# Linear attention and 16 routed experts on one core: fewer steps in a routing group, counts in bf16, and a new order of the first stage

## The chip, the cores and the metric

The program runs on one core of one Trainium2 chip. The metric is the device time of one execution in microseconds (us), the median of three runs. TensorE (PE), VectorE (DVE), ScalarE (ACT) and GpSimd (POOL) each work through a queue of their own in program order; SyncE (SP) issues most of the transfers, POOL those that scatter rows by an index.

## The reference, cut to what matters

```python
kv = einsum('bhsd,bhse->bhde', k, v)            # 8 batches, 8 heads, 576 rows, 64 wide
out = einsum('bhsd,bhde->bhse', q, kv)
x = out / sqrt(mean(out * out, -1) + 1e-6) * g_norm   # -> 4608 tokens of 512
g_idx, g_w = argmax and its softmax weight of x @ w_group        # 4 groups
e_idx, e_w = the same of x @ w_expert[g_idx]                     # 4 experts in each
y = g_w * e_w * (relu(x @ w1[g_idx, e_idx]) @ w2[g_idx, e_idx])  # 512 -> 1024 -> 512
```

Everything is float32. Each token goes to one of 16 experts.

## The kernel before, in words

**First stage: attention and routing.** The 4608 tokens are 36 tiles of 128. For each of the 8 batches SP loads k, v and q (8 x 3 MB and small tails, L516 and L528), PE forms kv, and for each tile it forms the tile's output and router logits in one product (L598). ACT copies the output into a ring of 20 tiles (`xo`, L603), copies the logits (L541) and squares the output (L619); DVE sums the squares (L626). Tiles are routed in eight groups (`GS`): DVE and ACT compute 1/rms (L719 to L741), the logits (L751, L756), their maxima and one-hot marks (L762 to L793), the exponentials and the token's weight (L841 to L905). PE sums the one-hot marks into running ranks (`rk`, L802 to L808, with the count so far, `carry`, of float32), DVE turns ranks into row numbers (`keys`, L834), and POOL scatters each tile's rows (544 floats a token, 4 x 136) into a table in memory, `xs`, sorted by expert (L267; a put in what follows). Ahead of most puts POOL writes the token's number into the tile's columns `TOK` and up (L913); groups 3, 4 and 7 do this in one copy a group (L924).

**The early region.** After group 1 the fullest expert is picked. When groups 0 to 4 (24 tiles) have been put, SP reads 256 of this expert's rows back (L292), and while groups 5 to 7 are still routed, PE computes the expert for these 256 tokens (first layer L363, second layer L1258 in nine passes). Its weights come in four loads of 1 MB (L223); the first needs only the pick.

**The order of the first stage** is found by a planner in the kernel itself: each piece of work is a step with an engine, a cost, a rank and the steps that it needs; the planner plays the steps through with its own costs and latencies (`SAME`, `OTHER`), and where several steps of an engine could start, the lowest rank (`RANK`, `ROUTE`, `FOLD`, `LOADS`, ...) goes first. What comes out is the order of each engine's queue. In the planner a put takes 1.28, has its rows in memory 0.1 + 1.0 later, and a step on POOL may follow 1.2 after that. A tile's place in the ring may be written again when the put of the tile 20 before it has landed.

**Between the stages** the rest of the first expert's tokens (region 0, 128 rows) and the preparation of region 1 are written out by hand (from L1462): the read of region 0's rows (`read(0)`, L292 again), the read of region 1's (`read(1)`, L289, which needs the widths of `region_columns`, L1372), the splitting of float32 weights into a high and a low part (ACT L246, DVE L250), the last piece of the early region's second layer (`head_layer2`), region 0's first layer (from `xT`, `xTl`), the row limits (`row_bounds`, `bad`, `ridx`) and masks (`quarter_masks`).

**Second stage.** Regions 1 to 15, one expert each, in three products a tile of weights (L374, L375, L379). The tiles `xh`, `xl`, `hh`, `hl` that PE reads are laid from column 16 x `FIRST_X[r]` or 16 x `FIRST_H[r]` on. At the end the results are scattered into the output, and a loop for overflowing rows is passed by.

## Time and profile before

| | us |
|---|---|
| median of three runs (lowest, highest) | 530.22 (529.77, 530.44) |
| the profiled execution's own time | 530.08 |
| its span, first to last instruction | 528.4 |
| PE busy in the span | 514.4 (97%) |
| DVE, ACT, POOL busy | 398.8, 277.8, 258.3 |

The profiled execution lies 0.14 us under the median, and 1.7 us of its time lie outside the span. PE's busy time includes warming products without use (L447) in the first stage, so that its share does not say what bounds that stage.

### The profile page before, as it was taken

What the parts mean: (1) busy time and instruction counts of PE and PEld (TensorE: products, weight loads), DVE (VectorE), ACT (ScalarE), POOL (GpSimd) and SP (SyncE); (2) the same over time, 40 slices, a digit from 0 to 9 for tenths busy, and PEclk for the clock granted to TensorE, in tenths of its full rate; (3) what the DMA queues carried; (4) which work ended last, traced back from release to release, by engine and by line L of the source; (5) the groups of instructions that cost most, each with busy time, mean ns of one, the idle gap of its engine ahead of it and who ended that gap; (6) DMA issues with size and microseconds to landing.
All of it is one profiled execution on the core that took longest, in us unless ns stands there. A gap on an engine that the chain in (4) does not pass through costs nothing. (4 is left out here: it accounts for less than half of the span.)

```text
span 528.4 us, 12161 instructions
## 1 busy us (share of the span) xinstructions
PE 514.4 (97%) x4262; PEld 497.7 (94%) x4262; DVE 398.8 (75%) x852; ACT 277.8 (53%) x499; POOL 258.3 (49%) x356
## 2 busy tenths in 40 slices
PE   6899999999999999999999999999999999999995
PEld 3899998788899999999999999999999999999995
DVE  4259998978967887887877777877878777878760
ACT  0378888634653544455454454545554646556551
POOL 7002865461021745647584646455564738365271
PEclk9899999999999999999999999999999999999998
DMA  8999998946998374636856555565748384854010
GB/s 319 422 422 418 419 423 325 354 182 208 300 360 320 106 289 125 250 118 174 297 219 198 219 197 222 199 253 158 269 148 306 107 329 124 316 209 182 15 40 36
DMA packets 44026, 126.50 MB, mean 239 GB/s; under 512 B 6992, under 2 KB 26390, under 8 KB 32925
## 3 DMA queue, kind: packets, MB, share of 16 engines
q1 hardware_dynamic: 36029, 105.71, 54.5%
q0 software_dynamic: 7760, 19.48, 10.0%
q8 instruction: 62, 1.02, 0.8%
q14 instruction: 31, 0.25, 0.2%
q10 hardware_dynamic: 144, 0.04, 0.1%
HBM read 105.73 MB, written 20.51 MB: 239 GB/s over the span
## 5 line engine op out<-in xcount | busy, mean ns | idle before, releaser
L1438 POOL DMA_INDIRECT out_dram<-z,idx x140 | 164.3, 1173 | 155.4 <-DVE idx L1416 117.0
L375 PE MATMUL ps<-xl,whi 128*128 128x300 f32 (+12 forms) x480 | 141.5, 295 | 0.0
L374 PE MATMUL ps<-xh,whi 128*128 128x300 f32 (+12 forms) x480 | 141.3, 294 | 0.0
L379 PE MATMUL ps<-xh,wlo 128*128 128x300 f32 (+12 forms) x480 | 141.3, 294 | 0.0
L375 PE MATMUL psy<-hl,w2h 128*128 128x300 f32 (+11 forms) x448 | 133.0, 297 | 0.0
L374 PE MATMUL psy<-hh,w2h 128*128 128x300 f32 (+11 forms) x448 | 132.9, 297 | 0.0
L379 PE MATMUL psy<-hh,w2l 128*128 128x300 f32 (+11 forms) x448 | 132.6, 296 | 0.0
L250 DVE TENSOR_TENSOR wlo<-wr,whi 128x1024 fp32r<-128x1024 f32 x64 | 97.2, 1522 | 22.2 <-ACT whi L246 22.1
L379 PEld LDWEIGHTS ps<-xh,wlo 128*128 128x128 f32 x480 | 90.3, 188 | 0.0
L375 PEld LDWEIGHTS ps<-xl,whi 128*128 128x128 f32 x480 | 90.3, 188 | 0.0
L374 PEld LDWEIGHTS ps<-xh,whi 128*128 128x128 f32 x480 | 90.3, 188 | 0.0
L324 ACT ACTIVATE hh<-ps 128x328 fp32r<-128x328 f32 (+11 forms) x120 | 50.4, 420 | 74.5 <-PE ps L379 73.7
L352 DVE TENSOR_TENSOR w2l<-wr,w2h 128x1024 fp32r<-128x1024 f32 x60 | 73.4, 1224 | 18.9 <-ACT w2h L348 18.1
L379 PEld LDWEIGHTS psy<-hh,w2l 128*128 128x128 f32 x448 | 84.3, 188 | 0.0
L375 PEld LDWEIGHTS psy<-hl,w2h 128*128 128x128 f32 x448 | 84.2, 188 | 0.0
L374 PEld LDWEIGHTS psy<-hh,w2h 128*128 128x128 f32 x448 | 84.2, 188 | 0.0
L348 ACT CAST w2h<-wr 128x1024 fp32r<-128x1024 f32 x60 | 62.5, 1042 | 38.7 <-PE psy L375 35.3
L325 DVE SCALAR_TENSOR_TENSOR hl<-ps,hh 128x328 fp32r<-128x328 f32 (+11 forms) x120 | 55.6, 463 | 23.3 <-ACT hh L324 23.2
L1430 ACT ACTIVATE xh<-xt,rw 128x328 fp32r<-128x328 f32 (+11 forms) x60 | 32.6, 544 | 68.6 <-DVE xt L311 68.6
L246 ACT CAST whi<-wr 128x1024 fp32r<-128x1024 f32 x64 | 66.3, 1037 | 1.3 <-DMA wr<-in_w_dram 1.3
L267 POOL DMA_INDIRECT xs<-xo,keys x36 | 35.7, 991 | 31.4 <-DVE pt L751 10.3
L321 POOL TENSOR_TENSOR xq<-xq 128x1280 f32<-128x1280 f32 (+3 forms) x14 | 33.9, 2419 | 18.1 <-DMA xq<-xs 17.9
(302 smaller groups left out, 671.9 us busy)
## 6 DMA issues: line engine op xcount, KB each, us to landing
wr<-in_w_dram SPq DMA_DIRECT2D x64, 1024.0 KB
m_q<-in_qm_dram SPq DMA_DIRECT2D x8, 1024.0 KB
m_k<-in_k_dram SPq DMA_DIRECT2D x7, 1024.0 KB
m_v<-in_v_dram SPq DMA_DIRECT2D x7, 1024.0 KB
xq<-xs SPq DMA_DIRECT2D x20, 153.0 KB
out_dram<-z,idx POOLq DMA_INDIRECT x140
xq<-xs SPq DMA_DIRECT2D x16, 136.0 KB
xq<-xs SPq DMA_DIRECT2D x12, 119.0 KB
```

What stands on the lines that cost most here:

```text
L246: nc.scalar.copy(out=hi, in_=w)
L250: eng.tensor_tensor(out=lo, in0=w, in1=hi.bitcast(F32), op=ALU.subtract)
L267: sc = nc.gpsimd.indirect_dma_start(out=xs, out_offset=bass.IndirectOffsetOnAxis(ap=keys[:, c:c + 1], axis=0), in_=x.rearrange("p i f -> p ...
L321: eng.tensor_tensor(out=part(x, n), in0=part(x, n), in1=factors(x, n), op=ALU.mult)
L324: nc.scalar.activation(out=hh, in_=ps, func=AF.Relu)
L325: nc.vector.scalar_tensor_tensor(out=hl, in0=ps, scalar=0.0, in1=hh.bitcast(F32), op0=ALU.max, op1=ALU.subtract)
L348: nc.scalar.copy(out=piece(hi, hf, i2), in_=halfpiece(wt[hf][0], i2))
L352: nc.vector.tensor_tensor(out=piece(lo, hf, i2), in0=halfpiece(wt[hf][0], i2), in1=piece(hi, hf, i2).bitcast(F32), op=ALU.subtract)
L374: nc.tensor.matmul(ps, lhsT=stat_h(c), rhs=mov_h(c), start=(c == 0), stop=False)
L375: nc.tensor.matmul(ps, lhsT=stat_h(c), rhs=mov_l(c), start=False, stop=False)
L379: nc.tensor.matmul(ps, lhsT=stat_l(d), rhs=mov_h(d), start=False, stop=(d == n - 1))
L1438: sc = nc.gpsimd.indirect_dma_start(out=out4, out_offset=bass.IndirectOffsetOnAxis(ap=idx[:, g:g + 1], axis=0), in_=z[:, g, :], in_offset= ...
```

## The change

A routing group loses the step `m` (ACT takes the mean and the 1e-6 into the logarithm), the step that adds 1e-9 to `se` (now part of the two steps behind it) and `carry`. The counts so far are kept as bf16 counts a partition (`counted`), summed by one reduction a group, and PE adds them with two bf16 products in place of the float32 one. POOL writes the token numbers of every group in one copy, which needs only that the ring's places are free. The groups are 5 and 3 tiles where they were 4 and 4 (groups 3 and 4). The 256 early rows are read in two transfers, and the first of the expert's weights is loaded behind them. The ranks are new. Between the stages `region_columns` moves into the first stage, `row_bounds` and the masks move behind region 0's products, `head_layer2` gets the bank of `ps_e`, and one weight split goes ahead of `xTl`. `FIRST_X` and `FIRST_H` change in four places, and one constant of 512 bytes a partition is gone, so that the tiles behind it lie elsewhere.

```diff
-FIRST_X = [0, 0, 0, 0, 2, 2, 2, 0, 0, 0, 2, 2, 0, 1, 1, 0]
-FIRST_H = [0, 0, 0, 0, 0, 0, 0, 2, 2, 2, 1, 1, 1, 1, 1, 0]
-
-
-GS = [6, 5, 5, 4, 4, 5, 4, 3]
+FIRST_X = [0, 0, 0, 0, 2, 2, 2, 0, 0, 0, 2, 1, 0, 1, 1, 0]
+FIRST_H = [0, 0, 0, 0, 0, 1, 1, 2, 2, 1, 1, 1, 1, 1, 1, 0]
+
+
+EARLYIDS = -30.0
+
+
+GS = [6, 5, 5, 5, 3, 5, 4, 3]
...
-RANK = {'hl': 25.95, 'wh': 39.35, 'wd': 636.8, 'ek': -2962.18, 'o': 5229.48, 'ok': 34.12, 'sq': 7956.27, 'red': 2.73, 'w': -2197.5, 'wl': 2652.43, 'wl2': -2193.01, 'xt': -587.87, 'xs': 18.38, 'l1': 10123.65, 'hs': -14.64, 'l2': 58.33, 'lk': 9.34}
...
+ROUTE = [0.98, 5.63, -0.45, 4.95, 44.06, 5.6, -21.59, -24.17]
+FOLD = [327.49, -98.1, -44.42, 3.17, 1.83, -24.19, -89.66, -194.68]
...
-    ones_f = cp.tile([1, P], F32, name="ones_f")
+    g2 = cp.tile([P, 1], F32, name="g4")
+    tiny = cp.tile([P, 1], F32, name="tiny")
+    base_b = cp.tile([P, NE], BF16, name="base_b")
...
+    def read_tokens(x, row, nb, eng, head=False, j=0):
+        d = eng.dma_start(x.rearrange("p j i f -> p (j i f)"), xs[bass.ds(row, P * nb), :][j * P:(j + 1) * P])
...
+    ps_e = both.enter_context(tc.tile_pool(name="ps_e", bufs=1, space=bass.MemoryType.PSUM))
...
-                nc.vector.tensor_scalar(out=tl([H], "m"), in0=mss[g][:, 0:nt, :].rearrange("p t h -> p (t h)"),
-                                        scalar1=1.0 / D, scalar2=1e-6, op0=ALU.mult, op1=ALU.add)
-            s = do("D", nt * H, [done["red", c] for c in cols] + [get("end", g - 2)], f)
-
-            def f():
-                nc.scalar.activation(out=tl([H], "lnm"), in_=v["m"], func=AF.Ln)
-            s = do("A", nt * H, [s], f, us=0.25)
+                v["ms"] = mss[g][:, 0:nt, :].rearrange("p t h -> p (t h)")
+                nc.scalar.activation(out=tl([H], "lnm"), in_=v["ms"], func=AF.Ln, scale=1.0 / D, bias=tiny[:, 0:1])
+            s = do("A", nt * H, [done["red", c] for c in cols] + [get("end", g - 2)], f, us=0.25)
...
+                v["seen"] = counted[g % 2]
+                nc.vector.tensor_tensor(out=v["seen"][:, 1:1 + nt, :], in0=v["oh3"],
                                         in1=sign.unsqueeze(1).to_broadcast([P, nt, NE]), op=ALU.mult)
-                v["ohs3"] = v["ohs"].rearrange("p (t e) -> p t e", e=NE)
-            s1 = do("D", nt * 16, [s1, done["constants"]], f)
+            s1 = do("D", nt * 16, [s1, done["constants"], get("rk", g - 2), get("seen", g - 2)], f)
...
                 rk = v["rk"] = ps_r.tile([P, 512], F32, name="rk", tag="psr")
-                nc.tensor.matmul(rk[:, 0:nb_], lhsT=ones_f, rhs=st["carry"].unsqueeze(1).to_broadcast([1, nt + 1, NE]),
-                                 start=True, stop=False)
-                for t in range(nt):
-                    nc.tensor.matmul(rk[:, (t + 1) * NE:nb_], lhsT=ones_b,
-                                     rhs=v["ohs3"][:, t, :].unsqueeze(1).to_broadcast([P, nt - t, NE]), start=False,
-                                     stop=False)
-                nc.tensor.matmul(rk[:, 0:nt * NE], lhsT=upper_b, rhs=v["ohs"], start=False, stop=True)
+                for t in range(-1, nt + 1):
+                    x = base_b if t < 0 else v["seen"][:, t, :]
+                    m = nt + 1 - max(t, 0)
+                    nc.tensor.matmul(rk[:, max(t, 0) * NE:nb_], lhsT=ones_b,
+                                     rhs=x.unsqueeze(1).to_broadcast([P, m, NE]), start=(t < 0), stop=False)
+                nc.tensor.matmul(rk[:, 0:nt * NE], lhsT=upper_b, rhs=v["seen"][:, 1:1 + nt, :].rearrange("p t e -> p (t e)"),
+                                 start=False, stop=True)
                 v["tot"] = rk[:, nt * NE:nb_]
-            rk = do("PE", 0, [s1, done["carry", g - 1], get("kr", g - 1), get("tot", g - 1)], f, us=0.1 + 0.065 * nt)
-
+            rk = done["rk", g] = do("PE", 0, [s1, get("seen", g - 1), get("kr", g - 1), get("tot", g - 1)], f,
+                                    us=0.12 + 0.055 * nt)
+
+            if not last:
+                def f():
+                    with nc.allow_low_precision(reason="a partition's tokens number at most 36"):
+                        nc.vector.tensor_reduce(out=counted[(g + 1) % 2][:, 0, :],
+                                                in_=v["seen"][:, 0:nt + 1, :].rearrange("p t e -> p e t"), op=ALU.add,
+                                                axis=AX.X)
+                done["seen", g] = do("D", nb_, [s1, get("rk", g - 1)], f)
 
             def f():
                 nc.vector.tensor_tensor(out=tl([NE], "kr"), in0=v["rk"][:, 0:nt * NE], in1=v["ohb"], op=ALU.mult)
-            kr = done["kr", g] = do("D", nt * 16, [rk], f)
+            kr = cnt = done["kr", g] = do("D", nt * 16, [rk], f)
...
-                    carry = sm.tile([1, NE], F32, name="carry", bufs=2)
-                    nc.vector.tensor_copy(out=carry, in_=v["tot"][0:1, :])
-                    st["carry"] = carry
-                cnt = done["carry", g] = do("D", NE, [rk], f)
...
-                    nc.vector.tensor_scalar(out=v["se"], in0=v["se"], scalar1=1e-9, scalar2=None, op0=ALU.add)
...
+            eng, e = (nc.vector, "D")
+
+            def f():
+                nc.vector.tensor_reduce(out=tl([5], "se"), in_=v["ex"], op=ALU.add, axis=AX.X)
+                v["se5"] = v["se"].rearrange("p (t s) -> p t s", s=5)
+            w = do("D", nt * 20, [w], f)
+
+            def f():
+                nc.vector.scalar_tensor_tensor(out=tl([1, 4], "s4"), in0=v["se5"][:, :, 1:5], scalar=1e-9,
+                                               in1=v["oh5"][:, :, 0, :], op0=ALU.add, op1=ALU.mult)
+            w = do("D", nt * 4, [w], f)
+
+            def f():
+                nc.vector.tensor_reduce(out=tl([1], "s1_"), in_=v["s4"], op=ALU.add, axis=AX.X)
+            w = do("D", nt * 4, [w], f)
+
+            def f():
+                nc.vector.scalar_tensor_tensor(out=tl([1], "cw"), in0=v["se5"][:, :, 0], scalar=1e-9, in1=v["s1_"],
+                                               op0=ALU.add, op1=ALU.mult)
+            w = do("D", nt, [w], f)
...
-            def put(c):
-                nc.gpsimd.tensor_copy(out=xot[c][:, :, TOK:REC].bitcast(I32),
-                                      in_=tok4[:, c, :].unsqueeze(2).to_broadcast([P, 4, REC - TOK]))
-                put_rows(c, xot[c])
-
-            us = 1.58
-            put_all = last or g in (EARLY - 1, EARLY)
-            if put_all:
-                def f():
-                    for lo, hi in [(0, min(nt, XO - r0)), (min(nt, XO - r0), nt)]:
-                        if hi > lo:
-                            at = (r0 + lo) % XO
-                            nc.gpsimd.tensor_copy(
-                                out=ring[:, at:at + hi - lo, :, TOK:REC].bitcast(I32),
-                                in_=tok4[:, c0 + lo:c0 + hi, :].unsqueeze(3).to_broadcast([P, hi - lo, 4, REC - TOK]))
-                ids = do("G", nt * 60, [done["ok", c] for c in cols], f)
-                us, put = 1.28, lambda c: put_rows(c, xot[c])
+            def f():
+                for lo, hi in [(0, min(nt, XO - r0)), (min(nt, XO - r0), nt)]:
+                    if hi > lo:
+                        at = (r0 + lo) % XO
+                        nc.gpsimd.tensor_copy(
+                            out=ring[:, at:at + hi - lo, :, TOK:REC].bitcast(I32),
+                            in_=tok4[:, c0 + lo:c0 + hi, :].unsqueeze(3).to_broadcast([P, hi - lo, 4, REC - TOK]))
+            ids = step("G", cost("G", nt * 60), cols[0] + EARLYIDS, [get("in", c - XO) for c in cols], f)
 
             for c in cols:
-                prev = do("G", 0, [w, ids if put_all else None, ks, done["sq", c], prev], lambda c=c: put(c), us=us)
+                prev = do("G", 0, [w, ids, ks, done["sq", c], prev], lambda c=c: put_rows(c, xot[c]), us=1.28)
...
+            x = do("D", 32, [x], f, us=0.2)
+            done["srow"] = do("D", 32, [x], region_columns, us=1.0)
             return cnt
 
         def early_region(do, rows):
             xq0 = ap_.tile([P, HEAD // P, 4, REC], F32, name="xq0", bufs=1)
 
-            def f():
-                read_tokens(xq0, first_row(star_row), HEAD // P, nc.sync, head=True)
             s = do("W", 0, rows + [done["star_row"]], lambda: None, us=1.0)
-            s = do("S", 0, [s], f, us=2.8)
+            st["read"] = []
+            for j in range(HEAD // P):
+                def f(j=j):
+                    if j == 0:
+                        st["row"] = first_row(star_row)
+                    read_tokens(xq0[:, j:j + 1], st["row"], HEAD // P, nc.sync, head=True, j=j)
+                s = do("S", 0, [s], f, us=1.41)
+                st["read"].append(s)
...
-                               ([] if i == 0 else [wt[-1], st["read"]]) + [done["star_idx"]], f,
+                               ([] if i == 0 else [wt[-1]]) + [st["read"][-1], done["star_idx"]], f,
...
-                s = step("D", 0.62, r0 + RANK["xt"] + 0.1 * j, [st["read"]], f, take=1 if j == 0 else 0)
+                s = step("D", 0.62, r0 + RANK["xt"] + 0.1 * j, [st["read"][j]], f, take=1 if j == 0 else 0)
...
-            for n, (j, hf, x) in enumerate([(j, 0, x) for x in (0, 2, 1) for j in range(2)] + [(0, 1, x) for x in (0, 2, 1)]):
+            for n, (j, hf, x) in enumerate([(0, 0, 0), (1, 0, 0), (0, 0, 2), (1, 0, 2), (0, 1, 0), (0, 1, 2), (0, 0, 1), (1, 0, 1), (0, 1, 1)]):
...
-                carry = sm.tile([1, NE], F32, name="carry", bufs=2)
-                nc.vector.tensor_copy(out=carry, in_=ekey[0:1, :])
-                st["carry"] = carry
-            done["carry", -1] = done["constants"] = step("D", 0.1, 3, [s], f)
+                for i in range(2):
+                    counted.append(sm.tile([P, GMAX + 1, NE], BF16, name=f"counted{i}"))
+                nc.vector.memset(counted[0][:, 0, :], 0.0)
+                nc.vector.tensor_scalar(out=counted[0][0:1, 0, :], in0=odd[0:1, :], scalar1=-1.0, scalar2=None,
+                                        op0=ALU.mult)
+                nc.vector.tensor_scalar(out=base_b, in0=middle, scalar1=1.0 / P, scalar2=None, op0=ALU.mult)
+            done["seen", -1] = done["constants"] = step("D", 0.3, 3, [s], f)
...
+        psy = [ps_q.tile([P, 512], F32, name=f"psy{d}") for d in range(3)]
+        psy.append(ps_e.tile([P, 512], F32, name="psy3", tag="pse"))
-        region_columns()
...
+        ids0 = mp.tile([P, 1], F32, name="ids0", bufs=1)
+        nc.vector.tensor_copy(out=ids0, in_=xqs[0][:, 0, TOK:TOK + 1])
+        o = psy[3][:, 0:DM // 2]
...
-            split_low(w1r[1], q, nc.vector)
-        row_bounds()
...
+        split_low(w1r[1], 0, nc.vector)
...
+        split_low(w1r[1], 1, nc.vector)
...
-        for _ in quarter_masks():
-            pass
...
+        row_bounds()
+        bad = [mp.tile([P, 3], F32, name=f"bad{i}", bufs=1) for i in range(2)]
...
+        for _ in quarter_masks():
+            pass
```

## Rows read from the trace of the kernel before

**Rows 1.** The profile's page, its second part, DMA busy tenths in 40 slices of 13.2 us.

```profile
DMA  8999998946998374636856555565748384854010
```

**Rows 2.** Windows: start:end, length, then busy us of PE, PEld, DVE, ACT, POOL, PEclk, DMA share, GB/s.

```profile
93.00:103.00 10.00, 9.63 (x60) 6.93 (x55) 9.86 (x46) 6.53 (x17) 4.09 (x7) 1.00 0.97 354
...
140.26:522.56 382.30, 382.30 (x2858) 381.31 (x2856) 292.40 (x464) 192.72 (x297) 200.10 (x156) 1.00 0.57 202
```

**Rows 3.** DMA queues from 3 to 91 us: packets, MB, share.

```profile
q1 hardware_dynamic: 6998, 29.20, 80.9%
q0 software_dynamic: 1920, 6.69, 18.7%
```

**Rows 4.** DMA queue of the puts, from 50 us to 62.79 and to 77.77.

```profile
q0 software_dynamic: 362, 1.28, 24.6%
...
q0 software_dynamic: 1014, 3.56, 31.4%
```

**Rows 5.** Timeline of SP's issues: start us, us, line, transfer.

```profile
58.11 0.35 SPq L223 DMA_DIRECT2D wr<-in_w_dram  x1
...
91.64 0.40 SPq L292 DMA_DIRECT2D xq<-xs  x1
...
118.10 0.34 SPq L292 DMA_DIRECT2D xq<-xs  x1
...
121.87 3.90 SPq L289 DMA_DIRECT2D xq<-xs  x8
```

**Rows 6.** Timeline of POOL: start us, us, line, operation, idle before.

```profile
50.54 1.18 POOL L267 DMA_INDIRECT xs<-xo,keys  x1 [7.66 <-DVE ex L766]
...
77.77 0.97 POOL L267 DMA_INDIRECT xs<-xo,keys  x1 [1.68 <-issue]
...
86.70 0.97 POOL L267 DMA_INDIRECT xs<-xo,keys  x1 [0.30 <-ACT xr L541]
...
99.05 0.22 POOL L913 COPY xo<-tok 128x16 int32<-128x16 int32 x1
...
114.80 0.98 POOL L267 DMA_INDIRECT xs<-xo,keys  x1 [0.30 <-issue]
```

**Rows 7.** Timeline of PE in the early region.

```profile
98.37 5.34 PE L363 MATMUL l<-xx,wr 128*128 128x256 f32 x24
...
103.65 0.44 PE L802 MATMUL rk<-carry,ones_f 1*128 1x80 f32 x2
```

**Rows 8.** Timeline of DVE in the last groups' routing.

```profile
100.72 0.17 DVE L719 TENSOR_SCALAR m<-ms 128x24 f32<-128x24 f32 x1
...
104.51 0.15 DVE L821 COPY carry<-rk 1x16 f32<-1x16 f32 x1
...
104.79 0.21 DVE L834 TENSOR_REDUCE keys<-kr 128x4 int32<-128x64 f32 x1
...
108.53 0.17 DVE L852 TENSOR_SCALAR se<-se 128x15 f32<-128x15 f32 x1
```

**Rows 9.** Timeline of DVE and PE between the stages.

```profile
121.03 0.69 DVE L302 TENSOR_TENSOR xn<-xq 128x512 f32<-128x512 f32 x1 [0.32 <-DMA xq<-xs]
...
123.36 0.39 PE L374 MATMUL ps<-whi,hhi 128*128 128x256 f32 x1 [0.46 <-ACT xx L1276]
...
126.76 0.39 PE L374 MATMUL ps<-lc,lb 128*128 128x512 f32 x1
...
130.81 1.76 DVE L321 TENSOR_TENSOR xq<-xq 128x1536 f32<-128x1536 f32 x1 [0.24 <-DMA wr<-in_w_dram]
...
134.27 0.39 PE L379 MATMUL ps<-whi,la 128*128 128x256 f32 x1 [1.19 <-DVE la L1533]
```

**Rows 10.** Timeline of PE, first products of two regions 300 wide.

```profile
256.18 0.30 PE L374 MATMUL ps<-xh,whi 128*128 128x300 f32 x1
...
269.30 0.30 PE L374 MATMUL psy<-hh,w2h 128*128 128x300 f32 x1
...
282.73 0.30 PE L374 MATMUL ps<-xh,whi 128*128 128x300 f32 x1
```

112 lines of the change are left out of this document (30 added, 82 removed).

## The prediction, made before the changed kernel was run

> **What bounds the kernel now.** I read the page first, then windows by stage, the transfers, and last the timelines around the seam between the stages. [rows 1] show the transfer engines full until about 80 us and then falling. In [rows 2] the second stage, from 140.26 to 522.56 us, has PE busy 382.30 of 382.30 us: no wait is left in it, and the time behind it (528.4 less 522.56, 5.8 us) is the last scatter, which the change doesn't touch. So a gain must bring region 1's first product forward from 140.26, or make the products themselves quicker.
>
> Two chains meet ahead of region 0's first layer, at 126.76 [rows 9].
>
> The first is PE's own: the early region starts at 98.37 [rows 7], 6.7 us after its rows are read at 91.64 [rows 5], and PE has little idle time from there on. The read waits for 24 puts. From 3 to 91 us the queues moved 29.20 MB of loads and 6.69 MB of puts [rows 3], 35.9 MB in 88 us, 0.41 MB/us: they are full, and the last bytes to arrive are those of the puts. One of the 29 MB is the expert's first weight half, issued at 58.11, ahead of the last q [rows 5].
>
> The second is that of the last put: issued at 114.80 [rows 6], followed by the read of region 0's rows at 118.10 [rows 5], and DVE takes these up at 121.03, after an idle time that ends with the transfer [rows 9]. From there DVE needs 5.7 us of splits to what PE starts with at 126.76. What makes the last put late is DVE: from 93 to 103 us it is busy 9.86 of 10 us [rows 2].
>
> **The change, part by part.**
>
> *Weight behind the read.* 1.05 MB less ahead of the puts' last bytes, at 0.41 MB/us: the read can go out 2.5 us earlier, at 89.1. It is not lost again: the weight is then behind two small reads, and the first product needs it 6 us after the read's issue; the transfer takes 2.5 of these. Lower bound 0 (if the puts are issued so late that the queue runs empty), upper 2.5.
>
> *Read in two transfers.* The first half's scaling and transposes no longer wait for the second half. 0.56 MB take 1.3 us, half of them 0.65; DVE's scaling of a half is 0.69, as that of region 0's rows [rows 9]. Bounds 0 and 0.65; I take 0.5. The second issue on SP stands ahead of weights only.
>
> *Counts.* The float32 product with `carry` takes PE 0.44 us [rows 7]; two small bf16 products take its place, which this trace doesn't show at that size. Bounds 0 and 0.44 a group, 0.3 taken; two such groups lie inside the early region's first layer: 0.6.
>
> *DVE steps.* A group loses `m` (0.17), the 1e-9 step (0.17) and `carry` (0.15) and gains a reduction; the nearest row is that of `keys`, 0.21 [rows 8]. That is 0.28 a group, 0.85 for the last three, in the stretch where DVE is full. In the last group's chain two of the steps were links: ACT's logarithm no longer waits for `m`, about 0.2, and the 1e-9 step's place is worth 0.17 and the hop behind it, 0.25 in all. With the new ranks the fold may also stand ahead of the rank's return rather than behind it, up to 1.2; I take half of that, 0.6. Sum for the last put: 0.85 + 0.2 + 0.25 + 0.6 = 1.9, taken as 2.0; bounds 0 (another order eats it) and 4, if this chain follows PE's.
>
> *Between the stages.* PE waits 0.46 us at 123.36 for a bank that ACT empties [rows 9]; in `ps_e` it needn't. It waits 1.19 at 134.27 for DVE [rows 9]. That DVE step stands behind the scaling of region 1's rows (130.81, 1.76 us), which had just arrived, and they were asked for only at 121.87, 3.8 us behind the read at 118.10 [rows 5], because DVE computed the widths after four weight splits. With `region_columns` in the first stage the second read follows the first at once, and with `row_bounds` and the masks moved, about 3 us of DVE work leave the way. So both waits should go: 0.46 on PE's chain, 1.19 behind both chains. What is late next is DVE's part of region 1, with those 3 us as cover; the moved masks are first needed by region 1's row numbers, some ten us later, and POOL's scatter of region 0 behind `ridx` holds only puts of results, which nothing waits for. Reading the ids into `ids0` keeps `read(2)` free of that delay on SP.
>
> *Laying `xh` to `hl` elsewhere.* The rows are 96 products each: 269.30 - 256.18 = 13.12 us for 300 columns in one place, 282.73 - 269.30 = 13.43 in another [rows 10]. So one place is worth 0.31 us a layer. Four entries change, and every tile moves with the constant that went. I take 0: the same number of layers can win as lose. Bounds: two layers at the better rate, -0.6, and four at the worse, +1.2.
>
> *Ids in one copy.* A copy ahead of a put takes 0.22 us on POOL [rows 6] with an issue gap of about as much. Inside the first 24 puts that shortens POOL's queue, but the puts' bytes are behind anyway (next), so I count it at nothing.
>
> **The sum.** PE's chain: 2.5 + 0.5 + 0.6 + 0.46 = 4.1, its first layer for region 0 at 122.7. The last put's chain: 2.0, at 124.8. The later one counts: 2.0, and 1.19 behind it, 3.2 us. Against the profiled execution's 530.08 that is 526.9; the median lies 0.14 above: 527.0.
>
> **Rivals.**
>
> *A, slower: the early ids copies hold POOL.* The copy of a group is now ready, for the planner, as soon as the puts 20 tiles earlier count as landed, 1.28 + 0.1 + 1.0 + 1.2 = 3.6 us after a put's start. The chip is far slower there. A put is 80 packets (1920 for 24 [rows 3]). At 77.77, as the 17th put goes out [rows 6], 1014 have moved, 12.7 puts, so 3.3 are waiting; between 62.79 and 77.77 the queue moved 652 packets, 8.2 puts in 15 us, 1.8 us each [rows 4]. A put thus lands some 4.3 x 1.8 = 8 us after its issue, and a copy that stands early in POOL's queue holds all puts behind it for up to 4.4 us. Five groups (3 to 7) have such a copy. POOL's slack: from 50.54 to 86.70 + 1.28 are 37.4 us [rows 6], and 24 puts need 30.7, so 6.7. Three full waits are 13.2, 6.5 too many: the last early put goes out at 93.2, its rows are read 3.3 us later (as at 114.80 and 118.10) at 96.5, 4.9 late; less 0.5, 0.6, 0.46 and 1.19 that is 2.1 slower, 532.3. It decides from a read later than 94.4, that is a put later than 91.1, two and a half waits. Against it: the copies may stand where POOL is idle anyway (7.66 us before the first put [rows 6]), and an earlier start of the puts would pay for them. On the price of a landing the Trainium skill ("DMA: Bandwidth & Descriptors", section "Anatomy of one DMA — SWDGE (gpsimd) path") has a rule: a transfer of POOL's costs about 2 us and its bytes at 436 GB/s, for these 0.28 MB an estimate of 2.6 us. By that no copy would wait at all, and this rival would fall away; the packets that are still waiting in [rows 4] speak against it while the loads run, and the 3.3 us from put to read at the end of the stage [rows 5, 6] come close to it when they don't.
>
> *B: only the seam.* The new order leaves the last put where it was; then 1.19 alone comes off, 529.0. For it: PE's gain is hidden behind the other chain. Against: DVE is full there and loses work.
>
> *C: both chains in full.* The last put follows the earlier loads as well; PE's 4.1 count, and 1.19: 5.3, 524.9.
>
> **How the numbers follow.** Less than 0.2% (1.06 us) either way is about what a measurement of this kernel cannot tell from no change. I give the forecast 0.42, A 0.24, B 0.19, C 0.15. Faster: 0.42, C and half of B, 0.66; the same: the other half of B and a small A, 0.12; slower: 0.22. The range takes in most of C and A's smaller half: 524.5 to 531.8; the likeliest case's own is 525.6 to 529.0: the bounds of the places, -0.6 and +1.2, and 0.8 either way for the last put.
>
> **What would show it.** The early read (two issues of L292's successor) at 89 to 90 and PE's first early product at 95 to 96; the last put at 112 to 113.5, the widths computed before the read of region 0, no idle time of PE over 0.3 us between region 0's first layer and region 1; region 1's first product near 137; the stretch from there to PE's last product 382 us within one. Wrong: POOL idle for several us ahead of a copy of ids, with puts behind it, and a read later than 92; or a stretch of regions 1 to 15 longer than 383.

## The result and the profile after

The changed kernel takes 537.22 us (536.18 to 537.84) where the kernel before takes 530.33 on the same chip (529.77 to 530.66): ratio 1.0126, 95% interval 1.0112 to 1.0140. It is 6.9 us slower; the forecast was 3.2 us faster. The profiled execution has a span of 535.4 us. Eight further runs fell on executions with a mean granted clock of 0.94 to 0.97, in which the kernel before took 568 to 612 us, and no verdict is read from their times.

I read the second stage first. Windows of the changed kernel, columns as in [rows 2]:

```profile
93.00:103.00 10.00, 3.08 (x18) 1.96 (x16) 2.69 (x12) 2.03 (x5) 1.42 (x2) 0.79 0.67 230
147.63:530.23 382.60, 382.60 (x2858) 381.61 (x2856) 292.80 (x479) 192.76 (x297) 199.69 (x156) 1.00 0.58 202
```

Regions 1 to 15 take 382.60 us, against 382.30 [rows 2]. So the loss lies ahead of region 1's first product, at 147.63 instead of 140.26: 7.37 later. (Behind PE's last product 5.2 us are left, against 5.8.) And from 93 to 103 us, where DVE was busy for 9.86 of 10 us, it is now busy for 2.69. Something stands still there. The timeline of POOL shows what:

```profile
54.56 0.20 POOL L899 COPY xo<-tok 128x16 int32<-128x16 int32 x1 [3.15 <-DMA xs<-xo,keys]
...
62.24 0.22 POOL L899 COPY xo<-tok 128x48 int32<-128x48 int32 x1 [2.00 <-DMA xs<-xo,keys]
...
64.33 0.97 POOL L272 DMA_INDIRECT xs<-xo,keys  x1 [0.30 <-ACT sq L634]
...
71.92 0.27 POOL L899 COPY xo<-tok 128x80 int32<-128x80 int32 x1 [4.04 <-DMA xs<-xo,keys]
...
81.59 0.24 POOL L899 COPY xo<-tok 128x64 int32<-128x64 int32 x1 [4.02 <-DMA xs<-xo,keys]
...
85.30 0.23 POOL L899 COPY xo<-tok 128x48 int32<-128x48 int32 x1 [0.69 <-DMA xs<-xo,keys]
...
93.75 0.98 POOL L272 DMA_INDIRECT xs<-xo,keys  x1 [0.31 <-ACT xr L556]
...
121.33 1.89 POOL L272 DMA_INDIRECT xs<-xo,keys  x1 [0.30 <-DMA xs<-xo,keys]
123.53 1.97 POOL L272 DMA_INDIRECT xs<-xo,keys  x1 [0.31 <-issue]
```

L899 are the copies of ids, L272 the puts. Each of the groups 3 to 7 has a copy that waits for a transfer of `xs`, that is for a put of 20 tiles earlier to land: 3.15 + 2.00 + 4.04 + 4.02 + 0.69 = 13.9 us, with all later puts behind it in POOL's queue. The copy at 71.92 (group 5, up to tile 28) needs the put of tile 8, issued at 64.33: 7.6 us. The planner counted 3.6. The last of these waits is short, and the loads run out at about 82 us: the copy at 85.30 needs the put issued at 82.35, 3.0 us before. The 24th put leaves at 93.75 instead of 86.70 [rows 6], although the first left 3.2 us earlier (47.35, against 50.54).

SP's issues, DVE and PE in the same trace show how far that reaches:

```profile
96.75 0.90 SPq L297 DMA_DIRECT2D xq<-xs  x2
98.23 2.47 SPq L228 DMA_DIRECT2D wr<-in_w_dram  x4
...
127.81 0.33 SPq L297 DMA_DIRECT2D xq<-xs  x1
129.35 3.88 SPq L294 DMA_DIRECT2D xq<-xs  x8
...
99.73 0.69 DVE L306 TENSOR_TENSOR xx<-xq 128x512 f32<-128x512 f32 x1 [7.43 <-DMA xq<-xs]
...
106.36 0.68 DVE L641 TENSOR_REDUCE ms<-sq 128x8 f32<-128x512 f32 x1
...
130.76 0.69 DVE L306 TENSOR_TENSOR xn<-xq 128x512 f32<-128x512 f32 x1 [3.12 <-DMA xq<-xs]
...
105.57 5.47 PE L367 MATMUL l<-xx,wr 128*128 128x256 f32 x24 [0.32 <-DMA wr<-in_w_dram]
...
135.88 0.50 PE L383 MATMUL ps<-lc,lb 128*128 128x512 f32 x1 [1.43 <-DVE lb L1480]
```

The early read is issued at 96.75 instead of 91.64 [rows 5]. DVE's queue has the scaling of these rows ahead of routing work for the last three groups, so DVE waits 7.43 us for them, and the squares' sums of the last group's tiles start at 106.36. From there the last put (123.53, against 114.80), the read of region 0's rows (127.81, against 118.10) and their scaling (130.76, against 121.03 [rows 9]) are 8.7 to 9.7 us late. Region 1's read follows region 0's after 1.5 us, as forecast, where it took 3.8.

### The profile page after: what moved, and what is told of

It reads as the page before. It is cut to its first block, busy times and chain, and to the rows that moved or that the text cites. A ratio compares the mean times of both kernels' runs of the same rounds, so it can differ in the third digit from the quotient of the medians.

```text
span 535.4 us, 12106 instructions
## 1 busy us (share of the span) xinstructions
PE 512.9 (96%) x4252; PEld 495.7 (93%) x4256; DVE 396.8 (74%) x842; ACT 278.1 (52%) x499; POOL 256.3 (48%) x337
## 5 line engine op out<-in xcount | busy, mean ns | idle before, releaser
L255 DVE TENSOR_TENSOR wlo<-wr,whi 128x1024 fp32r<-128x1024 f32 x64 | 94.6, 1482 | 21.5 <-ACT whi L251 21.5
L1403 ACT ACTIVATE xh<-xt,g 128x328 fp32r<-128x328 f32 (+11 forms) x60 | 32.6, 544 | 64.5 <-DVE xt L315 64.5
L272 POOL DMA_INDIRECT xs<-xo,keys x36 | 37.6, 1046 | 25.5 <-DVE ms L641 12.4
L613 PE MATMUL ops<-kvx,m_q 128*128 128x168 f32 x256 | 41.6, 313 | 0.8 <-DMA m_q<-in_qm_dram 0.4
```

The costliest lines, as they stand in the source:

```text
L255: eng.tensor_tensor(out=lo, in0=w, in1=hi.bitcast(F32), op=ALU.subtract)
L272: sc = nc.gpsimd.indirect_dma_start(out=xs, out_offset=bass.IndirectOffsetOnAxis(ap=keys[:, c:c + 1], axis=0), in_=x.rearrange("p i f -> p ...
L613: nc.tensor.matmul(ops[c][lo:hi, pr, 0:XW], lhsT=qs[:, pr * step_ + at + lo:pr * step_ + at + hi], rhs=kx[:, pr, :], start=True, stop=True)
```

## The experiments

Unless said otherwise, times are medians, and the ratio is to the kernel before on the same chip.

**f1: the copies of ids at their puts.** The planned order stays; only the copy is issued later.

```diff
-            ids = step("G", cost("G", nt * 60), cols[0] + EARLYIDS, [get("in", c - XO) for c in cols], f)
+            copy = f
+            ids = step("G", cost("G", nt * 60), cols[0] + EARLYIDS, [get("in", c - XO) for c in cols], lambda: None)
...
-  lambda c=c: put_rows(c, xot[c]), us=1.28)
+  lambda c=c: (copy() if c == c0 else None, put_rows(c, xot[c])), us=1.28)
```

> The changed kernel with one thing moved: the copy of a group's ids stands on POOL right ahead of the group's first put instead of early; the planned order of every engine's other work is unchanged. Theory (the early copies hold POOL, the read of the early rows is late by what they hold, and DVE, whose queue has the scaling of these rows ahead of the last three groups' routing, waits with it): the waits ahead of the copies, 13.9 us in all, are gone; the 24th put goes out at 84 to 85 instead of 93.75, the early read at 88 to 89.5 instead of 96.75, DVE's idle time ahead of the scaling is under 2 us instead of 7.43, the last put goes out at 114 to 116 instead of 123.53, and the time is 528 to 530.5. Rival (the newly found order and the weight behind the read are what is slow; the copies only use time in which the transfer queues were full anyway): the read stays behind 94 and the time at 535 or above. An earlier run of this kernel fell on a chip whose TensorE clock was held at 0.94, on which the kernel before took 611 us; neither theory can be read from it.

530.66 us, ratio 1.0017 (1.0003 to 1.0031): 6.6 us less than the changed kernel, and the same as before within the 0.2% that can be told. The 24th put leaves at 85.02. Timelines of SP, PE, POOL and DVE:

```profile
89.78 0.90 SPq L297 DMA_DIRECT2D xq<-xs  x2
91.26 3.60 SPq L228 DMA_DIRECT2D wr<-in_w_dram  x4
...
98.02 5.42 PE L367 MATMUL l<-xx,wr 128*128 128x256 f32 x24 [1.43 <-DMA wr<-in_w_dram]
...
113.82 1.88 POOL L272 DMA_INDIRECT xs<-xo,keys  x1 [0.30 <-issue]
116.00 1.97 POOL L272 DMA_INDIRECT xs<-xo,keys  x1 [0.30 <-issue]
...
92.67 0.68 DVE L306 TENSOR_TENSOR xx<-xq 128x512 f32<-128x512 f32 x1
...
110.83 0.21 DVE L833 TENSOR_TENSOR kr<-rk,ohb 128x48 f32<-128x48 f32 x1 [1.08 <-PE rk L818]
...
113.64 4.62 DVE L255 TENSOR_TENSOR wlo<-wr,whi 128x1024 fp32r<-128x1024 f32 x4
```

DVE no longer waits for the early rows (92.67, no idle time shown). Between this trace and that of the changed kernel everything moves together: the read by 6.97, the first scaling by 7.06, the first early product, the last put and region 1's first product (140.10) by 7.5 each. So the early copies cost, once, about what they hold back the read: 7.0 to 7.5 us in these traces, 6.6 in the medians. The theory holds; its last put (114 to 116) came at the upper end, its read (88 to 89.5) and its time (528 to 530.5) just above.

**f2: the early copies alone, in the kernel before.** The same copy for every group in place of the copies ahead of single puts.

```diff
-                ids = do("G", nt * 60, [done["ok", c] for c in cols], f)
+            ids = step("G", cost("G", nt * 60), cols[0] + EARLYIDS, [get("in", c - XO) for c in cols], f)
```

> The kernel before with one part of the change alone: each group's ids in one copy that may stand as early as the planner finds the 20-tile ring free, as in the changed kernel. Its ranks, weights and steps are those of before. Theory: POOL waits ahead of copies for 6 us or more in all, the 24th put goes out 3 to 7 us later than 86.70, the early read later than 94.4, and the kernel is slower: 532 to 537. Rival (order and weights are the cause): the time stays within 1 us of before.

544.21 us, ratio 1.0262 (1.0243 to 1.0281): 14 us slower, where 2 to 7 were expected. Timeline of POOL:

```profile
63.36 0.24 POOL L917 COPY xo<-tok 128x64 int32<-128x64 int32 x1 [5.94 <-DMA xs<-xo,keys]
...
75.99 0.25 POOL L917 COPY xo<-tok 128x80 int32<-128x80 int32 x1 [5.62 <-DMA xs<-xo,keys]
...
83.58 0.24 POOL L917 COPY xo<-tok 128x64 int32<-128x64 int32 x1 [1.97 <-DMA xs<-xo,keys]
87.25 0.22 POOL L917 COPY xo<-tok 128x48 int32<-128x48 int32 x1 [1.94 <-DMA xs<-xo,keys]
```

The waits sum to 15.5 us, the 24th put leaves at 97.12 (10.4 late, expected 3 to 7) and the early read at 100.07, 8.4 late. That early copies hold POOL and the read is shown in both orders. The 14 us are not all shown to be that: the planner makes another order of this kernel, with 32 products of the early layer instead of 24 ahead of a rank product, and from the read on it loses more (the last put, at 127.35, is 12.6 late). In the new order the copies cost half as much.

**h2: only the steps between the stages moved, in the kernel before** (`region_columns` in the first stage, `psy[3]` in `ps_e`, `ids0`, the split ahead of `xTl`, row bounds and masks last).

```diff
-            done["srow"] = x = do("D", 32, [x], f, us=0.2)
+            x = do("D", 32, [x], f, us=0.2)
+            done["srow"] = do("D", 32, [x], region_columns, us=1.0)
...
+        psy.append(ps_e.tile([P, 512], F32, name="psy3", tag="pse"))
...
-        region_columns()
```

> The kernel before with only the steps between the stages moved as in the changed kernel: the widths in the first stage, the fourth output bank of region 0 in the bank that lives through both stages, region 0's ids copied aside, the row bounds and masks behind region 0. Ranks, steps, weights, reads and copies are those of before. Theory: from the scaling of region 0's rows to region 1's first product it takes 16.9 us, as in the changed kernel with its copies at their puts, instead of 19.23; the time is 527.8 to 528.8. Rival (the rows of region 1 or DVE's splits hold region 1 as before): 529.7 or above.

528.53 us, ratio 0.9969 (0.9958 to 0.9981): 1.7 us faster. Timeline of DVE and PE:

```profile
122.39 0.69 DVE L302 TENSOR_TENSOR xn<-xq 128x512 f32<-128x512 f32 x1 [0.15 <-issue]
...
139.46 0.33 PE L374 MATMUL ps<-xh,whi 128*128 128x360 f32 x1
```

From the scaling of region 0's rows to region 1's first product it takes 17.07 us, where before it took 140.26 - 121.03 = 19.23. The changed kernel has 16.87 and f1 16.89. Along PE, from its first early product (99.69) to region 1's, it takes 39.77 instead of 41.89, 2.1 less; regions 1 to 15 take 382.74 instead of 382.30, 0.4 more. (In this profiled execution the whole first stage lies some 1.4 us late: ACT copies the first tile's output at 23.42, against 22.06; its own time was 529.53.)

**h1: the rest of the change in the old order.** The changed kernel with the old `GS` and ranks, late copies of ids, and the first weight free to go ahead of the read.

```diff
-GS = [6, 5, 5, 5, 3, 5, 4, 3]
+GS = [6, 5, 5, 4, 4, 5, 4, 3]
...
+            ids = do("G", nt * 60, [done["ok", c] for c in cols], f)
...
-                               ([] if i == 0 else [wt[-1]]) + [st["read"][-1], done["star_idx"]], f,
+                               ([] if i == 0 else [wt[-1], st["read"][-1]]) + [done["star_idx"]], f,
```

> The changed kernel with the groups' sizes and all ranks of the kernel before, the copies of ids needing their tiles' values (so that they stand late) and the first weight half free to be loaded ahead of the read. What is left of the change: fewer DVE steps, counts in bf16, the read in two transfers, the order between the stages, xh to hl elsewhere. Theory (the steps taken out shorten the last put's chain by about 2 us, as the prediction had it, and the new order and the weight gave that back): the last put goes out at 113 to 114 instead of 114.80, region 0's rows are scaled at 119 to 120.3, region 1 starts at 136.5 to 138, and the time is 526.5 to 528.5. Rival (the steps taken out were not on that chain: DVE waits there for PE's rank product, which stands behind a piece of the early layer): the last put stays within 0.5 of 114.80, and only the order between the stages pays: 528 to 529.5.

529.20 us, ratio 0.9981 (0.9972 to 0.9990). The rival holds: h2 has the order between the stages alone and is not slower, so fewer DVE steps, bf16 counts and the read in two transfers together gain nothing in this order. Timeline of DVE and POOL, and PE's rank product of the last group:

```profile
95.19 0.69 DVE L306 TENSOR_TENSOR xx<-xq 128x512 f32<-128x512 f32 x1 [0.51 <-DMA xq<-xs]
...
97.69 0.68 DVE L306 TENSOR_TENSOR xx<-xq 128x512 f32<-128x512 f32 x1
...
108.46 0.20 DVE L805 TENSOR_TENSOR counted<-ohb,sign 128x48 bf16<-128x48 bf16 x1
...
111.07 0.21 DVE L833 TENSOR_TENSOR kr<-rk,ohb 128x48 f32<-128x48 f32 x1 [0.71 <-PE rk L818]
...
115.11 0.98 POOL L272 DMA_INDIRECT xs<-xo,keys  x1 [0.30 <-ACT hhi L1208]
...
110.85 0.18 PE L818 MATMUL rk<-counted,upper_b 128*128 128x48 bf16 x1
```

DVE has the last group's marks ready at 108.66 and gets the ranks at 111.0, since PE has 24 products of the early layer ahead of the rank product. That wait is not new. The timeline of DVE in the kernel before has it too:

```profile
110.19 0.21 DVE L814 TENSOR_TENSOR kr<-rk,ohb 128x48 f32<-128x48 f32 x1 [1.09 <-PE rk L808]
```

The marks were ready at 107.74 there, so time saved on DVE ahead of them could only lengthen this wait. And with two transfers the two scalings are two steps, between which the planner put other work: they start 2.5 us apart, where before they ran back to back, and PE's early layer starts at 100.07 (98.37 before [rows 7]), 1.7 later. So "nothing" is a sum: what the counts save on PE (below), the late second scaling takes away again.

**g2: in f1, one split between the stages behind `xTl`**, which PE waited for.

```diff
-        split_low(w1r[1], 0, nc.vector)
...
-        split_low(w1r[1], 1, nc.vector)
+        for q in range(2):
+            split_low(w1r[1], q, nc.vector)
```

> The changed kernel with the copies of ids at their puts (530.66 in the run before this one) and one more step moved: between the stages DVE splits the first quarter of region 0's second weight half behind the second half of its rows (the step that writes xTl), not ahead of it. In the trace without this move PE waits 1.45 us at 128.33 for that step. Theory (the rows behind the last put set region 0's start and PE sets region 1's): PE's idle time there falls below 0.5, region 1's first product comes 0.8 to 1.2 earlier than 140.10, and the time is 529.4 to 530.0. Rival (DVE's work for region 1 ends last, its last step ending at 139.9): under 0.3 us, and PE waits later instead.

529.68 us (527.87 to 532.91), ratio 0.9997 (0.9980 to 1.0014). From the scaling to region 1's first product it takes 139.42 - 123.73 = 15.69 instead of 16.89, 1.2 less, and PE's wait of 1.45 is down to 0.26. Region 1 starts only 0.7 earlier than in f1 (expected 0.8 to 1.2), since the scaling is 0.5 later, and the runs spread too far for the time to confirm it.

**i4: in g2, the last group's rank product one piece of the early layer earlier.**

```diff
-  x + [free.pop(0), wt[f_ // 4], done["o", NTL - 1]], f)
+  x + [free.pop(0), wt[f_ // 4], done["o", NTL - 1]] + ([done["rk", len(groups) - 1]] if f_ >= 6 else []), f)
```

> The kernel of g2 (529.68) with the last group's rank product one piece of the early layer earlier in PE's queue: three pieces between it and the product of the group before, not four. Theory (DVE has the counts ready at 108.7 and waits for PE until 110.8; the last put's chain, which goes through this product, ends last at region 0): the product starts at 108.7 to 109.3 instead of 111.0, the last put goes out 1.4 to 1.9 earlier than 116.59, PE's idle time of about 1.1 ahead of region 0's transposes goes, and the time is 0.8 to 1.5 below g2's: 528.2 to 528.9. Rival (DVE's own steps make the last put late): the last put moves by less than 0.5 and the time by less than 0.3.

528.05 us (527.52 to 528.10), ratio 0.9952 (0.9940 to 0.9963): faster than both kernels, and the lowest median of all. Timelines of POOL, DVE, PE:

```profile
99.64 0.98 POOL L272 DMA_INDIRECT xs<-xo,keys  x1 [13.74 <-DVE ms L641]
...
113.77 0.97 POOL L272 DMA_INDIRECT xs<-xo,keys  x1 [0.30 <-issue]
115.04 0.98 POOL L272 DMA_INDIRECT xs<-xo,keys  x1 [0.30 <-issue]
...
115.52 4.61 DVE L255 TENSOR_TENSOR wlo<-wr,whi 128x1024 fp32r<-128x1024 f32 x4
...
137.50 0.32 PE L378 MATMUL ps<-xh,whi 128*128 128x360 f32 x1
```

The last put goes out 1.55 us earlier than in g2 (116.59). Little of that is the rank itself: the third put from the end moves by 0.54 (112.48, against 113.02). The rest is that the last two puts now leave before DVE's weight splits start (115.52; in g2 114.23), and take 0.97 and 0.98 us instead of 1.98 and 1.97.

**i2: the same rank step in h2.** 

> The kernel of h2 (before, with the new order between the stages; 528.53) with the last group's rank product one piece of the early layer earlier in PE's queue. In h2 region 0's first layer starts 4.98 us behind the scaling of its rows, against 3.05 where that chain binds, so PE's own chain, from its early start at 99.69, should end last. Theory: the last put goes out 1.2 to 1.8 earlier than 116.12, and the time stays within 0.5 of h2's. Rival (the last put's chain binds there too): 0.8 to 1.5 faster, 527.0 to 527.7.

528.67 us, ratio 0.9968 (0.9956 to 0.9981): no different from h2, as expected. The last put moves from 116.12 to 114.33, but 1.14 of that is there already at group 5's first put (98.26, against 99.40). The step itself is worth 0.65, not the expected 1.2 to 1.8: POOL is the limit there, and from group 5's first put on it now issues without a pause.

**Three misses, each of an edit that moved more than was meant.** g4 is g2 with the first weight free to go ahead of the read (the last change in h1's diff).

> The kernel of g2 with the expert's first weight half free to be loaded ahead of the early read again, as in the kernel before. Theory (with the copies at their puts, the weight behind the read is what is late: PE waits 1.43 us for it at 98.02, ACT's first Relu waits for PE, the squares of the last tile stand behind that Relu, and DVE's means, the last group's routing and the last put are late with them): PE starts the early region with no wait for the weight, the last put goes out 0.8 to 1.5 earlier than 116.0, and the time is 0.7 to 1.5 below g2's. Rival (the 1.05 MB ahead of the puts' last bytes hold the read back by as much as PE's wait was): the early read goes out 1.5 to 2.5 later than 89.78, PE starts no earlier than 97.5, and the time is within 0.4 of g2's.

538.53 us, ratio 1.0164 (1.0151 to 1.0177). With the new ranks the weight also passes loads of k and v (timeline of SP), and routing is late from there on.

```profile
57.90 0.35 SPq L228 DMA_DIRECT2D wr<-in_w_dram  x1
58.91 0.42 SPq L531 DMA_DIRECT2D m_k<-in_k_dram  x1
```

i3 is f1 with the first weight tied to the last load of q (`[done["load", B - 1, "q", 0]]`).

> The kernel of f1 (changed, copies of ids at their puts; 530.66) with the first weight half loaded right behind the last load of q, thus ahead of the early read, but ahead of no load of the first stage. Theory (the queues are full until the read, so the 1.05 MB cost the read what PE's wait for the weight cost behind it): the early read goes out 1.5 to 2.5 later than 89.78, PE's early layer starts within 0.7 of 98.02, and the time stays within 0.6 of f1's. Rival (the read waits for the puts' issue, not for bytes): the read stays within 0.7 of 89.78, PE starts at 96 to 97, and the time is 1 to 2 below f1's.

535.10 us, ratio 1.0091 (1.0076 to 1.0106). The read went out at 91.56, 1.8 later, as the theory had it; but the last small load of q slid behind the read's first half, and PE waited for it:

```profile
95.17 1.36 PE L613 MATMUL ops<-kvx,tail_q 128*64 128x168 f32 x16 [2.52 <-DMA tail_q<-in_qt_dram]
```

So what the weight alone is worth, ahead of the read or behind it, stays open; a third placing of it ran only among the eight runs without a verdict.

f4 is the changed kernel with the planner's wait for the early rows at 9.0 us in place of 1.0.

> The changed kernel (537.22), with the planner told that the early rows land 8 us later than it assumes, so that DVE's queue gets the scaling of these rows behind routing work instead of ahead of it; the ids copies still hold POOL. Theory: the read stays at 96 to 97, DVE's idle time ahead of the scaling falls below 2 us, the last put goes out 5 us or more earlier than 123.53, and PE's chain, which starts from the late rows, sets the end: 1 to 3 us faster than the changed kernel, 534 to 536. Rival (DVE's order alone makes the loss, the late read would be hidden): 529 to 531. An earlier run of this kernel fell on the chip whose TensorE clock was held at 0.94; neither theory can be read from it.

543.97 us, ratio 1.0257 (1.0235 to 1.0280). The last put did go out 8.2 us earlier, with the read as late as in the changed kernel (97.24). That fits DVE's place for the scaling as what made the put late, though the whole order is another one. This order put ACT's splits into `lc`, whose place the last puts still read, ahead of the early layer's Relus. Timelines of POOL, ACT and PE:

```profile
115.30 0.97 POOL L272 DMA_INDIRECT xs<-xo,keys  x1 [0.30 <-issue]
...
121.19 1.99 ACT L251 CAST lc<-wr 128x1024 fp32r<-128x1024 f32 x2 [3.54 <-DMA xs<-xo,keys]
...
127.85 2.29 PE L1237 MATMUL l<-whi,hhi 128*128 128x256 f32 x9 [2.72 <-ACT hhi L1208]
```

Neither expected time came, and how the price of the copies divides between PE's late rows and DVE's blocked queue is not settled.

**The eight runs without a verdict.** e1, e2 and e4 are the kernels of f1, f2 and f4, run first.

> The changed kernel with one thing moved: the copy of a group's ids stands on POOL right ahead of the group's first put instead of early; the planned order of every engine's other work is unchanged. Theory (the early copies hold POOL, the read of the early rows is late by what they hold, and DVE, whose queue has the scaling of these rows ahead of the last three groups' routing, waits with it): the waits ahead of the copies, 13.9 us in all, are gone; the 24th put goes out at 84 to 85 instead of 93.75, the early read at 88 to 89.5 instead of 96.75, DVE's idle time ahead of the scaling is under 2 us instead of 7.43, the last put goes out at 114 to 116 instead of 123.53, and the time is 528 to 530.5. Rival (the newly found order and the weight behind the read are what is slow; the copies only use time in which the transfer queues were full anyway): the read stays behind 94 and the time at 535 or above.

> The kernel before with one part of the change alone: each group's ids in one copy that may stand as early as the planner finds the 20-tile ring free, as in the changed kernel. Its ranks, weights and steps are those of before. Theory: POOL waits ahead of copies for 6 us or more in all, the 24th put goes out 3 to 7 us later than 86.70, the early read later than 94.4, and the kernel is slower: 532 to 537. Rival (order and weights are the cause): the time stays within 1 us of before.

> The changed kernel, with the planner told that the early rows land 8 us later than it assumes (its wait after the puts 9.0 instead of 1.0 us), so that DVE's queue gets the scaling of these rows behind routing work instead of ahead of it; the ids copies still hold POOL. Theory: the read stays at 96 to 97, DVE's idle time ahead of the scaling falls below 2 us, the last put goes out 5 us or more earlier than 123.53, and PE's chain, which starts from the late read, then sets the end: 1 to 3 us faster than the changed kernel, 534 to 536. Rival (DVE's order alone makes the loss, the late read would be hidden): 529 to 531.

They took 620.81, 608.06 and 612.07 us, where the kernel before took 610.95, with runs from 590 to 626. In e1 no copy waits for a transfer and in e2 four copies wait 14.7 us in all, as in f1 and f2, but the late products of the first stage hide what follows from it: the last of q's end at 113 to 114 us, the reads go out at 107.16 and 106.85. e3 is the changed kernel with the first weight free, as in g4.

> The changed kernel with the expert's first weight half free to be loaded ahead of the early read again, as in the kernel before. In the changed kernel PE's first early layer, at 105.57, ends a wait for that weight. Theory (the last put's chain is as late as PE's): PE's early layer starts at 103 to 104, region 0 still waits for rows that are read behind the last put at 123 to 124, and the time moves by less than 1 us from 537.2. Rival (the weight behind the read is what costs): 534 to 535.

613.81 us: no verdict. j1 and k1 are one kernel, i4 with the weight tied to the last small load of q (`[done["tail", "q", NG - 1]]`), and j2 and k2 are i4 with the old `FIRST_X` and `FIRST_H`.

> The kernel of i4 (changed, copies of ids at their puts, DVE's step between the stages and the rank product moved; 528.05) with the first weight half loaded behind the last load of the first stage and ahead of the early read. Theory (until the read the queues are full, so 1.05 MB ahead of it cost the read what PE's wait for the weight costs behind it): the early read goes out 1.3 to 2.5 later than 89.75, PE's early layer starts within 0.7 of 98.33, and the time is within 0.6 of i4's. Rival (the read waits for the issue of the puts, not for bytes): the read within 0.7 of 89.75, PE's early layer at 96.5 to 97.5, and the time 0.5 to 1.5 below i4's.

> The kernel of i4 with the places of xh to hl as in the kernel before (four entries). Theory (the new places cost the 0.3 us by which regions 1 to 15 are longer than before): from region 1's first product to PE's last 382.5 to 382.7 instead of 382.88, and the time 0.2 to 0.4 below i4's. Rival (another tile that moved does it, since the kernel of h2 has the old places and 383.03): the stretch stays at 382.8 to 383.1 and the time within 0.3 of i4's.

> The kernel of i4 (changed, copies of ids at their puts, DVE's step between the stages and the rank product moved; 528.05) with the first weight half loaded behind the last load of the first stage and ahead of the early read. Theory (until the read the queues are full, so 1.05 MB ahead of it cost the read what PE's wait for the weight costs behind it): the early read goes out 1.3 to 2.5 later than 89.75, PE's early layer starts within 0.7 of 98.33, and the time is within 0.6 of i4's. Rival (the read waits for the issue of the puts, not for bytes): the read within 0.7 of 89.75, PE's early layer at 96.5 to 97.5, and the time 0.5 to 1.5 below i4's.

> The kernel of i4 with the places of xh to hl as in the kernel before (four entries). Theory (the new places cost the 0.3 us by which regions 1 to 15 are longer than before): from region 1's first product to PE's last 382.5 to 382.7 instead of 382.88, and the time 0.2 to 0.4 below i4's. Rival (another tile that moved does it, since the kernel of h2 has the old places and 383.03): the stretch stays at 382.8 to 383.1 and the time within 0.3 of i4's.

613.46, 617.12, 578.33 and 573.14 us, where the kernel before took 611.59 (j) and 568.41 (k). The weight's worth stays open. The places' worth can be read from k2's trace, layer by layer (below).

## Why the prediction was wrong, step by step

**"Ids in one copy ... so I count it at nothing" is the step that failed.** It was 6.6 us. Its reason, "the puts' bytes are behind anyway", failed: a copy that waits for a landing holds back the later puts themselves, until the loads are over and the bytes no longer matter. Rival A had the mechanism and got its first links right: the 24th put at 93.2 (93.75), the read at 96.5 (96.75), a landing of 8 us (7.6). That the put's time fits so well is partly luck: five copies waited, 13.9 us in all, not three for 13.2; the first put left 3.2 us earlier, and the copies and other pauses took 3.1. By the rule of the Trainium skill ("DMA: Bandwidth & Descriptors", section "Anatomy of one DMA — SWDGE (gpsimd) path") no copy would have waited; the trace speaks against it while the loads run, and the 3.0 us of the put at 82.35 come close to it when they don't. The chance of 0.24 weighed a hope about an order (copies where POOL idles anyway) above rows (queues full to 80 us). And A's price, 2.1, netted the late read against four gains on PE, and followed PE's chain only; DVE's queue carried the same delay to the last put.

**"The later one counts: 2.0" took the wrong chain.** The 5.7 us from the scaling of region 0's rows to its first layer are not 5.7 us of splits: DVE splits for 2.35 of them, and meanwhile the rows wait for PE. Timelines of PE, before and in f1:

```profile
124.53 0.60 PE L1500 MATMUL ps<-ident,xn 128*128 128x128 f32 x4
...
124.00 0.63 PE L1475 MATMUL ps<-ident,xn 128*128 128x128 f32 x4 [1.14 <-ACT la L251]
```

Before, the rows are scaled by 121.72 and PE turns to them at 124.53, without a wait. In f1 PE waits, until 0.1 us after they are scaled (123.90), and from the scaling to the first layer it takes 126.26 - 123.21 = 3.05 us. So the last put's chain had some 2.7 us to spare before, and PE's set the end; i2, whose last put gains 0.65, is not faster.

**The last put, -2.0.** It got +1.2 without the copies (f1). "What makes the last put late is DVE" read DVE's busy time, not its queue's neighbours. DVE waits for PE's ranks (1.09 at 110.19, above), and in the kernel before POOL issues the last 12 puts almost without a pause from 98.08 on (timeline of POOL):

```profile
98.08 0.98 POOL L267 DMA_INDIRECT xs<-xo,keys  x1 [10.04 <-DVE pt L751]
```

From there to 114.80 [rows 6] are 11 intervals of 1.52 us on average. In i4 the first of these puts goes out at 99.64, behind the early rows' scaling, and 11 intervals of 1.28, the plain put, end at 113.7 at best; measured 115.04. One copy a group made the puts denser, and their later start took that back. DVE's removed steps lie ahead of a wait for PE that was there already (h1). f1's +1.2 are 0.29 for the start of the put before it and 0.91 for that put's own longer duration.

**PE's chain, -4.1.** The read came at 89.78 (forecast 89.1) once the copies were out of the way. The first early product came at 98.02, not at 95 to 96: PE waits 1.43 us for the weight, whose product starts 6.8 us after its issue at 91.26. The sentence that the transfer takes 2.5 of the 6 us there was false; three more weights go out right behind it, which may be why, but no run tried that. So 0.35 us of the 2.5 and 0.5 arrived; in h1 the read in two transfers cost PE a later start. The 0.6 for the counts was right. PE in f1:

```profile
103.28 0.20 PE L816 MATMUL rk<-base_b,ones_b 128*128 128x80 bf16 x1
...
103.49 7.15 PE L367 MATMUL l<-xx,wr 128*128 128x256 f32 x32
```

From a rank product's first part to the early layer's next product it takes 0.21 and 0.16 us (103.28 to 103.49, 110.47 to 110.63), where before it took 0.52 and 0.48 (103.65 to 104.17, 109.52 to 110.00): 0.63 less in two groups. With the bank's 0.46 and some 0.3 more on the way, PE comes to the products at 123.36 [rows 9] 1.73 us earlier (121.63), not 4.1.

**Between the stages, -1.65.** Right: h2, where both waits are gone, gains 1.7 (2.1 ahead of region 1, less 0.4 behind its start). In the changed kernel, where the rows of the last put set the pace, a wait came back in another place (1.43 at 135.88), because the split moved ahead of `xTl`; g2 takes it out.

**Places, 0 (-0.6 to +1.2).** 382.60 against 382.30, inside the bounds. But "one place is worth 0.31 us" compared a first layer with a second [rows 10]. i4 and k2 differ in the four entries alone, and the time of a layer, from its first product to the next layer's, repeats within 0.03 us in regions 1 to 9 of these two traces but for the layers with a new entry:

| layer, entry | k2, old place | i4, new place |
|---|---|---|
| region 5, second, 0 to 1 | 13.43 | 13.26 |
| region 6, second, 0 to 1 | 13.43 | 13.26 |
| region 9, second, 2 to 1 | 12.64 | 12.51 |
| region 11, first, 2 to 1 | 11.86 | 12.16 |

h2 has k2's four numbers within 0.01. Together the entries gain 0.17 us. The loss is older: h2 and i2, with the old entries, take 382.74, f2, with the old order between the stages, 382.30 like the kernel before. So it comes with that order (region 3's first layer takes 14.51 in h2 instead of 14.08); which of its moves does it, no run shows.

**The books.** Region 1 starts 7.37 later: 7.53 for the copies (changed kernel less f1), less 0.50 up to region 0's first layer without them (f1 126.26, against 126.76), 0.34 more behind it. The 0.50 is what is left of PE's 1.73: the scaling of region 0's rows comes 2.18 later in f1 (123.21, against 121.03: the last put 1.20, its own duration 0.99), and PE waits for it. In i4, region 1 starts at 137.50, 2.8 us before the old place. The rows' scaling at 121.15 is 0.1 behind its old place, so none of that comes from the last put: 1.35 lie on PE's chain up to region 0's first layer (125.41; the counts' 0.6 and the bank's 0.46 among them) and 1.41 behind it.

## What to carry to other kernels

An instruction that is ready early in a planner's model is not free in an in-order queue: price its wait by the trace's slowest landing, and charge it to everything behind it. Before a saving on a busy engine is counted, look at what its next consumer stands behind: DVE was busy for 9.86 of 10 us and still stood ahead of a wait for PE. Where two chains meet, look which of them waits for the other: rows that lie ready for 2.8 us are not late. Between two kernels, line up one event of each engine; equal shifts (here 7.0 to 7.5) point to one cause.

## What the hardware showed beyond expectation

In these traces a put that starts inside a DVE operation with two inputs in SBUF waits for that operation's end. Timeline of DVE in the changed kernel, the first of four weight splits:

```profile
121.16 1.22 DVE L255 TENSOR_TENSOR wlo<-wr,whi 128x1024 fp32r<-128x1024 f32 x1
```

It ends at 122.38; the put that started inside it at 121.33 takes 1.89 us on POOL and ends at 123.22, 0.84 later. Eight puts start inside a split: two each in the changed kernel, f1 and g2, one each in f2 and e1. They take 1.50 to 1.98 us, according to what is left of the split, and each ends 0.84 to 0.85 us after it. In f4 two puts start inside the early rows' scaling (L306, two inputs, 0.69 and 0.68 us from 100.57 and 102.34): they take 1.40 and 1.47 and end 0.84 to 0.85 after it. A put inside a sum with one input isn't held (88.63 in the changed kernel, DVE L641 from 88.61 to 89.29: 0.98 us), nor is one that starts ahead of the splits (the last put before, in h1, h2, i2, i3 and i4: 0.97 to 0.98, though in the kernel before a split began 0.28 after it). The Trainium skill ("SBUF — State Buffer", section "SBUF: two separate sides") says that of a DVE operation with two SBUF inputs and a GpSimd operation that reads SBUF the one that starts first keeps the port that they share until it ends; these rows agree with it, and the prediction had not used it. No run moved the splits alone.
